# Sorted-block attention before a gated FFN: batch 0 with queries transposed by token halves through an identity selection, keys on split blocks and mixed first, values mixed from strided weight columns

## The chip, the cores and the metric

The kernel runs on one core of a Trainium2 chip. Its metric is the device time of one execution in microseconds (us), lower is better. The core has five engines that run their own instruction streams and wait for one another by semaphores: TensorE (PE, with its weight loads shown apart as PEld), VectorE (DVE), ScalarE (ACT), GpSimd (POOL) and SyncE (SP). Transfers are issued here from POOL's queue (all loads, which also cast from float32 to bf16) and from SP's queue (the outputs and some transposes).

## What is computed

```python
P = sort_net                                   # [4, 8, 8, 8]: batch, head, block i, block j
for _ in range(5):                             # Sinkhorn
    P = exp(P); P = P / P.sum(-1); P = P / P.sum(-2)
k_sorted = einsum('bhij,bhjcd->bhicd', P, k_blocks)    # 8 blocks of 96 tokens, 64 wide
v_sorted = einsum('bhij,bhjcd->bhicd', P, v_blocks)
attn = softmax(q_blocks @ k_sorted.T / 8) @ v_sorted   # inside each block
x = attn with heads side by side                       # [3072, 512]
out = (silu(x @ w_gate) * (x @ w_val)) @ w_out         # 512 -> 1536 -> 512
```

Inputs and output are float32; there are 4 batches, 8 heads, 768 tokens and a head width of 64.

## The kernel before

The work runs batch by batch. A batch gives two token tiles of 384 tokens (half a batch, four blocks), so the FFN has eight tiles, n = 0 to 7. One tile is 12 pairs of `gate` (L351) and `value` (L369), each 4 matmuls of 384 columns into one PSUM bank, and 3 output groups of 12 matmuls (`outp`, L383). The attention of later batches is woven between these by `merge` (L547), which takes a cost for every FFN step and a due time for every side step. That weave is for PE and POOL only; DVE and ACT are ordered there by the framework. Ahead of it, up to L515, the order of PE, POOL, DVE and ACT is written out by hand, and that is the part in question: batch 0 has nothing to hide behind.

For batch 0 the stages are:

- **Loads** (L134 to L152), in POOL's order: the values in two halves, the identity matrix, the queries, the keys in four pieces, then POOL's share of the value copies, then a tiny copy named `landed` (L144) which holds POOL until the last key piece is there, then the FFN weights in steps of 256 columns, batch 1's values, keys and queries, and w_out. Values, keys and queries lie with (head, block j) on 64 partitions each; keys of batch 0 on partitions 0 to 63 and queries on 64 to 127 of one tile.
- **Value transposition** (`copy_v`, L117): POOL and ACT copy the values from "token, width" to "width, token" order into `vch`, so that the 96 tokens of one width column lie next to each other.
- **Sinkhorn** (L183 to L205): five iterations on DVE with an Exp on ACT in each. Between them sit the mask (L187), a copy of the identity into the mixing matrix (L188) and ACT's value copies (L190, L192, L206, L207). PE meanwhile runs matmuls on zeros: `dots(124)` and a few `fill` matmuls of 512 columns per iteration.
- **Mixing matrix**: 16 small matmuls (L432) spread the weights over partitions, and L439 masks them into `rmix`.
- **Mixing** (L449 to L464): `v_chunk` (L238) takes a width column of `vch` as weights and the mixing matrix as the moving operand; `kq_chunk` (L227) takes a token column of the joint key and query tile, so that keys are mixed and queries transposed by the same matmul (the identity part of `rmix`). Each chunk of 8 or 16 columns fills one or two PSUM banks, and DVE ("v") or ACT ("s") drains it to `vt` or `kqt`. PSUM has a two-bank tile "a", a two-bank tile "b", three single banks "gen" and one bank "x".
- **Attention** for units 0 to 3 (L469 to L489): `scores` and `exps` make the exponentials of one head pair and four blocks, `av` multiplies them with the mixed values and DVE divides by the sums (`r_sb` L308, `st` L310), `x_to` transposes the result on PE, and a drain puts it into x of tile 0. One unit gives one of the four 128-row pieces of x for all 384 tokens.
- **First FFN matmuls** (`early`, L492): gate(0), value(0) and gate(1) of tile 0, piece by piece as x arrives.

Thirteen `fill` matmuls (L414) stand between the mixing matrix and the first FFN matmuls. Units 4 to 7 of batch 0 (the tokens of tile 1) are woven into FFN tile 0 (L581), and batch 1 into tile 1.

## Time and profile before

| | |
|---|---|
| median of 3 runs | 250.0 us (249.75 to 250.14) |
| span of the profiled execution | 248.0 us; its own device time is not listed, so 2.0 us to the median stand for what lies around the span |
| PE busy | 240.1 us, 97% of the span, 2636 matmuls |
| DVE, ACT, POOL busy | 157.7, 110.3, 52.5 us |
| chain that ended last, by engine | PE 83%, DVE 7%, ACT 3%, DMA 2% |
| read from HBM | 28.3 MB; the DMA engines are nearly full up to about 85 us |

The span runs from the first to the last instruction, and times inside it are counted from its start. A row of the timeline is: start, length, engine, line, operation, tiles, how many instructions are merged, and in brackets how long the engine had been idle and what ended the wait. A row of the groups gives the busy time and the mean length of one instruction. Matmuls are pipelined, so the length of one says how long it was under way, not how far apart two of them start.

### The profile page before, as it was taken

What the parts mean: (1) busy time and instruction counts of PE and PEld (TensorE: products, weight loads), DVE (VectorE), ACT (ScalarE), POOL (GpSimd) and SP (SyncE); (2) the same over time, 40 slices, a digit from 0 to 9 for tenths busy, and PEclk for the clock granted to TensorE, in tenths of its full rate; (3) what the DMA queues carried; (4) which work ended last, traced back from release to release, by engine and by line L of the source; (5) the groups of instructions that cost most, each with busy time, mean ns of one, the idle gap of its engine ahead of it and who ended that gap; (6) DMA issues with size and microseconds to landing.
All of it is one profiled execution on the core that took longest, in us unless ns stands there. A gap on an engine that the chain in (4) does not pass through costs nothing.

```text
span 248.0 us, 6193 instructions
## 1 busy us (share of the span) xinstructions
PE 240.1 (97%) x2636; PEld 141.3 (57%) x2636; DVE 157.7 (64%) x332; ACT 110.3 (44%) x187; POOL 52.5 (21%) x47
## 2 busy tenths in 40 slices
PE   7899999999999999999999999999999999999994
PEld 6376566666555556655555655565555555555543
DVE  6778689887555775857657646755764585446700
ACT  2977553453544444454642552354244334232311
POOL 7948459960059200000000000000000000000000
PEclk9999999999999999999999999999999999999999
DMA  5959999999999296010122121112111121100122
GB/s 101 211 95 166 215 189 228 194 226 211 221 170 192 53 210 164 3 42 3 45 54 52 57 62 34 44 42 78 32 42 45 39 57 55 42 22 24 42 81 88
DMA packets 39530, 24.38 MB, mean 98 GB/s; under 512 B 27728, under 2 KB 35664, under 8 KB 38992
## 3 DMA queue, kind: packets, MB, share of 16 engines
q0 software_dynamic: 21328, 14.16, 38.9%
q1 hardware_dynamic: 18176, 9.84, 14.1%
q8 instruction: 20, 0.33, 0.5%
q14 instruction: 6, 0.05, 0.1%
HBM read 28.32 MB, written 7.86 MB: 146 GB/s over the span
## 4 chain that ended last, share of the span: by engine, by line
PE 83%; DVE 7%; ACT 3%; issue 3%; DMA 2%; DVEq 0%; ACTq 0%; POOLq 0%
PE v_ps L373 23%; PE o_ps L390 23%; PE g_ps L355 22%; PE tkq L233 4%; PE av_ps L304 3%; PE qk L277 2%; DVE gs_sb L365 2%; DMA v<-in_v_dram 2%; DVE st L310 2%; PE tv L245 2%; PE idle_ps L416 1%; DVE h L378 1%; PE o_ps L406 1%; ACT th_sb L363 1%; PE x_ps L321 1%
## 5 line engine op out<-in xcount | busy, mean ns | idle before, releaser
L365 DVE SCALAR_TENSOR_TENSOR gs_sb<-th_sb,g_ps 128x384 bf16<-128x384 bf16 x96 | 52.8, 550 | 51.8 <-ACT th_sb L363 49.1
L373 PE MATMUL v_ps<-xt,wv_sb 128*128 128x384 bf16 x380 | 77.3, 326 | 0.7 <-DVE gs_sb L365 0.4
L355 PE MATMUL g_ps<-xt,wg_sb 128*128 128x384 bf16 x376 | 76.5, 326 | 0.0
L363 ACT ACTIVATE th_sb<-g_ps 128x384 bf16<-128x384 f32 x96 | 47.1, 490 | 56.0 <-PE g_ps L355 53.5
L390 PE MATMUL o_ps<-wo_sb,h 128*128 128x512 bf16 x276 | 64.0, 379 | 0.0
L378 DVE SCALAR_TENSOR_TENSOR h<-v_ps,gs_sb 128x384 bf16<-128x384 f32 x96 | 53.3, 556 | 6.6
L373 PEld LDWEIGHTS <-wv_sb 128*128 128x128 bf16 x380 | 35.4, 97 | 24.6 <-issue 2.3
L355 PEld LDWEIGHTS <-wg_sb 128*128 128x128 bf16 x376 | 34.6, 97 | 23.2 <-issue 0.3
L390 PEld LDWEIGHTS <-h 128*128 128x128 bf16 x276 | 26.3, 98 | 28.9
L395 ACT COPY o_sb<-o_ps 128x512 f32<-128x512 f32 x23 | 13.5, 585 | 50.8 <-PE o_ps L390 50.8
L124 POOL COPY vch<-v 64x1536 bf16<-64x1536 bf16 (+2 forms) x11 | 28.6, 2639 | 20.7 <-DMA v<-in_v_dram 20.7
L290 ACT ACTIVATE e_all<-qk 96x768 bf16<-96x768 f32 x30 | 22.6, 802 | 8.1 <-PE qk L277 8.1
L310 DVE TENSOR_TENSOR st<-av_ps,r_sb 96x512 bf16<-96x512 f32 x32 | 21.7, 679 | 0.2
L304 PEld LDWEIGHTS <-e_all 96*128 96x128 bf16 x256 | 12.2, 98 | 4.9 <-ACT e_all L290 0.8
L304 PE MATMUL av_ps<-vt,e_all 96*128 96x65 bf16 x256 | 13.5, 194 | 0.0
L211 DVE CAST vt<-tv 96x1024 bf16<-96x1024 f32 (+1 forms) x9 | 9.8, 1100 | 2.7 <-PE tv L255 1.6
L308 DVE RECIPROCAL r_sb<-av_ps 96x8 f32<-96x8 f32 x32 | 6.4, 199 | 7.6 <-PE av_ps L304 7.5
L213 ACT CAST vt<-tv 96x1024 bf16<-96x1024 f32 (+1 forms) x9 | 9.2, 1032 | 3.1 <-PE tv L255 1.8
L211 DVE CAST kqt<-tkq 128x1024 bf16<-128x1024 f32 (+1 forms) x7 | 7.5, 1068 | 2.7 <-PE tkq L233 2.6
L213 ACT CAST kqt<-tkq 128x1024 bf16<-128x1024 f32 (+1 forms) x7 | 6.0, 894 | 6.6 <-PE tkq L233 6.6
L416 PE MATMUL idle_ps<-warm_sb 128*128 128x512 bf16 x28 | 8.7, 409 | 0.0
L233 PE MATMUL tkq<-rmix,kq 128*64 128x64 bf16 x384 | 7.8, 197 | 0.6 <-issue 0.6
(74 smaller groups left out, 126.3 us busy)
## 6 DMA issues: line engine op xcount, KB each, us to landing
out_dram<-o_sb SPq DMA_DIRECT2D x23, 256.0 KB, 2.0
v<-in_v_dram POOLq DMA_DIRECT2D x3, 768.0 KB, 19.9
kq<-in_q_dram POOLq DMA_DIRECT2D x2, 768.0 KB, 13.6
wg_sb<-in_moe_w_gate_dram POOLq DMA_DIRECT2D x6, 256.0 KB, 8.5
wv_sb<-in_moe_w_val_dram POOLq DMA_DIRECT2D x6, 256.0 KB, 9.1
wo_sb<-in_moe_w_out_dram POOLq DMA_DIRECT2D x1, 1536.0 KB, 23.8
kp<-in_k_dram POOLq DMA_DIRECT2D x2, 768.0 KB, 15.1
q_scr<-in_q_dram POOLq DMA_DIRECT2D x2, 768.0 KB, 29.9
```

The lines of the kernel that those rows point to most:

```text
L124: eng.tensor_copy(dst, src.transpose([0, 2, 1]))
L211: nc.vector.tensor_copy(dst, src)
L233: nc.tensor.matmul(tp[two * D:(two + 1) * D, lc, :], lhsT=kq_tiles[b][:, at + lc, :], rhs=rm[:, two], start=True, stop=True)
L290: nc.scalar.activation(e_all[:, n:n + 2, 0:4 * C], wide[0:C, :, 0:4 * C], AF.Exp, scale=scale)
L304: nc.tensor.matmul(o[:, two, i4, :], lhsT=e[:, i4 * C:i4 * C + 128], rhs=vt[:, 2 * g + two, half * 4 + i4, :], start=True, stop=True)
L310: nc.vector.tensor_tensor(st.rearrange("p i two d -> p two i d"), o[0:C, :, :, 0:D], r_sb.to_broadcast([C, 2, 4, D]), op=ALU.mult)
L355: nc.tensor.matmul(g_ps, lhsT=wg_sb[:, kc, ts(m, 128)], rhs=xt[:, kc, :], start=(kc == 0), stop=(kc == NKC - 1))
L363: nc.scalar.activation(th_sb, g_ps, AF.Tanh, scale=0.5)
L365: nc.vector.scalar_tensor_tensor(gs_sb, th_sb, 1.0, g_ps, op0=ALU.add, op1=ALU.mult)
L373: nc.tensor.matmul(v_ps, lhsT=wv_sb[:, kc, ts(m, 128)], rhs=xt[:, kc, :], start=(kc == 0), stop=(kc == NKC - 1))
L378: nc.vector.scalar_tensor_tensor(h_tiles[n][:, m, :], v_ps, 0.5, gs_tiles.pop(m), op0=ALU.mult, op1=ALU.mult)
L390: nc.tensor.matmul(o_ps, lhsT=h_w[:, m, ts(t3, 128)], rhs=wo_sb[:, m, :], start=(m == 0), stop=(m == NFC - 1))
```

## The change

It concerns batch 0 alone, apart from batch 1's value mixing, which now always multiplies all 128 rows, so that the lower half of `vch` is set to zero by POOL.

- **Loads**: first half of the queries (by tokens), the keys in two halves of their 96 tokens on the lower and the upper 64 partitions, the identity, the values as a whole (into a tile with room for 128 tokens, the last 32 set to zero), the second half of the queries, then the FFN weights at once and partly in larger steps. `landed` and all copies of batch 0's values are gone.
- **Queries** (`q0_chunk`): the 384 tokens of one half are 16 runs of 24, so that 8 heads by 16 runs lie on 128 partitions; a matmul on one of the 24 token columns, with identity columns as its moving operand, transposes the heads of one parity. The first half is transposed during Sinkhorn iteration 2 and drained by ACT in iterations 3 and 4; the second half (`q0_rest`) comes inside FFN tile 0.
- **Keys** (`k0_chunk`): 48 token columns with both halves on 128 partitions, mixed by a matrix of twice the width; they come before the values.
- **Values** (`v0_chunk`): the weights are read from the natural tile, 128 tokens with a step of 64 elements.
- **Units 0 to 3** (`blocks`): a unit is now four heads by two blocks, so that units 0 and 1 complete half of the tokens of tile 0 for all heads; the first FFN matmuls run on 192 columns at a time.
- The thirteen `fill` matmuls behind the mixing matrix are gone; the score matmuls of units 0 and 1 stand between value chunks.

The core of the diff (the moved helpers `drain`, `kqt_tile`, `kq_chunk`, `v_chunk` left out):

```diff
-    load_v(0, 0, HC)
-    load_v(0, HC, C)
+    q_runs = q.rearrange("b h (t j c) d -> b t h j (c d)", t=2, c=QC)
+    qk0 = natp.tile([128, C, D], BF16, name="qk0", tag="nat")
+    q0 = [qk0[:, HC + t * QC:HC + (t + 1) * QC, :] for t in range(2)]
+    k0 = qk0[:, 0:HC, :]
+    load_q0(0)
+    for a, rows in enumerate(halves):
+        nc.gpsimd.dma_start(out=k0[rows], in_=k_nat[0, :, a * HC:(a + 1) * HC, :])
     make_identity(nc, ident)
-    load_q(0, 0, C)
-    for lo, hi in ((0, 32), (32, 64), (64, 80), (80, 96)):
-        load_k(0, lo, hi)
-    copy_v(nc.gpsimd, 0, lowr, 0)
-    copy_v(nc.gpsimd, 0, lowr, 3)
-    copy_v(nc.gpsimd, 0, lowr, 5, 8, 40, D)
-    landed = const.tile([R, 1], BF16)
-    nc.gpsimd.tensor_copy(landed, kq_tiles[0][0:R, C - 1, D - 1:D])
-    for m in range(0, 1024, 256):
-        load_gv(m, m + 256)
+    load_v(0, 0, C)
+    nc.gpsimd.memset(v_tiles[0][lowr, C:], 0.0)
+    load_q0(1)
+    load_gv(0, 256)
+    load_gv(256, 512)
+    load_gv(512, 1024)
     load_v(1, 0, C)
-    for m in range(1024, DF, 256):
-        load_gv(m, m + 256)
+    load_gv(1024, DF)
+    nc.gpsimd.memset(vch[lowr, 0:D * C], 0.0)
...
+    def q0_chunk(t, at, n, tag):
+        dst = kqt_tile(0)[:, GI * C:2 * GI * C].rearrange("p (g t r c) -> p t g r c", g=H2, t=2, c=QC)[:, t]
+        sel = ident.rearrange("p (g two r) -> p two g r", g=H2, two=2)
+        tp = chunk_tile("tq0", n // 8, tag).rearrange("p (l g r) -> p l g r", l=n, g=H2)
+        for lc in range(n):
+            for two in range(2):
+                nc.tensor.matmul(tp[two * D:(two + 1) * D, lc], lhsT=q0[t][:, at + lc, :],
+                                 rhs=sel[:, two], start=True, stop=True)
+        return dst[:, :, :, at:at + n], tp.rearrange("p l g r -> p g r l")
+    def k0_chunk(at, n, eng, tag):
...
+                nc.tensor.matmul(tp[two * D:(two + 1) * D, lc].rearrange("p a (g i) -> p a g i", g=H2),
+                                 lhsT=k0[:, at + lc, :], rhs=rm[:, two], start=True, stop=True)
+        drain(eng, dst[:, :, :, at:at + n], tp.rearrange("p l a n -> p a n l"))
+    def v0_chunk(at, n, eng, tag):
...
+            nc.tensor.matmul(tp[:, ld, :], lhsT=v_tiles[0][lowr, :, at + ld], rhs=mix, start=True, stop=True)
+        m = n // len(eng)
+        for k, e in enumerate(eng):
+            part = slice(k * m, (k + 1) * m)
+            drain(e, vts[0][:, 0, :, at + k * m:at + (k + 1) * m], tp[0:C, part].transpose([0, 2, 1]))
...
-        if it == 1:
+        if it == 2:
             with nc.allow_low_precision("0/1 mask"):
-                nc.vector.tensor_reduce(mask, id4, axis=AX.XY, op=ALU.add)
-            nc.vector.tensor_copy(rmix[0][highr, 1].rearrange("p h i -> p (h i)"), ident[highr, highr])
-        if it == 2:
-            copy_v(nc.scalar, 0, lowr, 2, 8)
+                nc.vector.tensor_reduce(mask.rearrange("p a h -> p (a h)"),
+                                        ident.rearrange("p (n j) -> p n j", j=NB), axis=AX.X, op=ALU.add)
         if it == 3:
-            copy_v(nc.scalar, 0, lowr, 3, 8)
+            drain("s", *early_q[0])
+        if it == 4:
+            drain("s", *early_q[1])
...
+        if it == 2:
+            early_q = [q0_chunk(0, 0, 16, "b"), q0_chunk(0, 16, 8, "gen")]
...
-    fill(idle_ps, 1)
-    v_chunk(0, 0, 8, "v", "gen")
...
-    kq_chunk(0, 88, 8, "v", "gen")
...
+    mix_of(1)
+    k0_chunk(0, 8, "v", "gen")
+    k0_chunk(8, 8, "s", "gen")
+    k0_chunk(16, 16, "v", "a")
+    k0_chunk(32, 16, "s", "b")
+    v0_chunk(0, 8, "v", "gen")
+    v0_chunk(8, 16, "v", "a")
+    held = scores(0, 0, "gen")
+    v0_chunk(24, 16, "v", "b")
+    exps(0, 0, *held)
+    v0_chunk(40, 8, "s", "gen")
+    held = scores(0, 1, "gen")
+    v0_chunk(48, 16, "vs", "a")
+    exps(0, 1, *held)
+    mix_of(2)
+    mix_of(3)
+    av(0, 0, "a")
     qk(0, 2, "gen")
...
     av(0, 1, "b")
-    fill(idle_ps, 1)
+    qk(0, 3, "a")
...
+    x_first(0, "s", "x")
+    av(0, 2, "b")
+    x_first(1, "s", "gen")
...
+    early(0, range(NKC), 0)
+    av(0, 3, "a")
+    early(1, range(NKC), 0)
+    x_first(2, "s", "x")
+    early(2, range(NKC), 0)
+    x_first(3, "v", "x")
+    for n in range(3):
+        early(n, range(NKC), 1)
...
-    merge(ffn(0), units(0, range(4, 8), (0.0, 5.6)))
+    def q0_rest():
+        for at, n, eng, tag in ((0, 16, "s", "b"), (16, 8, "v", "a")):
+            drain(eng, *q0_chunk(1, at, n, tag))
+
+    merge(ffn(0), [(0.0, q0_rest)] + units(0, range(4, 8), (1.2, 6.4)))
```

## The prediction

> **What bounds the kernel now.** I read the busy time by stage first (each engine: us busy, instructions in brackets).
>
> ```profile
> core 0: us, PE busy (x) PEld busy (x) DVE busy (x) ACT busy (x) POOL busy (x), PEclk, DMA share, GB/s
> 12.30:20.24 7.94, 7.36 (x263) 5.87 (x263) 6.36 (x8) 5.58 (x9) 4.49 (x8) 1.00 0.74 115
> 20.24:27.24 7.00, 6.91 (x99) 4.17 (x99) 4.43 (x12) 4.85 (x9) 4.60 (x7) 1.00 1.33 174
> 27.24:45.10 17.86, 17.72 (x170) 10.99 (x168) 15.48 (x36) 8.22 (x16) 13.00 (x8) 1.00 1.24 212
> 45.10:246.00 200.90, 198.58 (x1945) 114.64 (x1943) 123.03 (x235) 84.00 (x144) 19.95 (x11) 1.00 0.43 82
> ```
>
> From 27.24 on TensorE (PE) has no gaps worth the name: the stretch of the first token tile is 17.72 busy of 17.86, and all after it 198.58 of 200.90. The change leaves that program alone, so whatever the time before 27.24 gains or loses, plus what is added inside the first tile, arrives at the end undiminished. The two stages before are different: PE looks busy there too, but 13 of its matmuls are fillers (L416). The engines that empty PSUM set the pace, as the timeline shows (start, length, engine, line, count, wait in brackets):
>
> ```profile
> 12.30 1.92 PEld L245 LDWEIGHTS <-vch 64*128 64x128 bf16 x64 [0.23 <-issue]
> 12.30 2.04 PE L245 MATMUL tv<-rmix,vch 64*128 64x64 bf16 x64
> 12.75 2.52 DVE L211 CAST vt<-tv 96x512 bf16<-96x512 f32 x3 [0.59 <-PE tv L245]
> 14.27 2.16 PE L233 MATMUL tkq<-rmix,kq 128*64 128x64 bf16 x112
> 18.18 1.89 DVE L211 CAST kqt<-tkq 128x1024 bf16<-128x1024 f32 x2 [0.99 <-PE tkq L233]
> 19.13 1.01 ACT L213 CAST kqt<-tkq 128x1024 bf16<-128x1024 f32 x1 [1.68 <-PE tkq L233]
> 20.24 0.54 PEld L277 LDWEIGHTS <-kqt 64*128 64x128 bf16 x24 [0.42 <-ACT kqt L213]
> 26.02 0.36 DVE L211 COPY xt<-x_ps 128x384 bf16<-128x384 bf16 x1 [0.47 <-PE x_ps L321]
> ```
>
> Values are mixed from 12.30, keys and queries from 14.27, the last drain ends at 20.14 and scores start at 20.24. The drain of the last piece of x ends at 26.38; I call this moment D. PE still owes 0.86 us of early gate work then, and value(0,1) starts at 27.24 = D+0.86.
>
> Unit prices, from the groups by form of 12 to 27.2 us (behind the bar: us busy, then the mean length in ns):
>
> ```profile
> L310 DVE TENSOR_TENSOR st<-av_ps,r_sb 96x512 bf16<-96x512 f32 x4 | 2.7, 686 | 0.1
> L211 DVE CAST kqt<-tkq 128x1024 bf16<-128x1024 f32 x2 | 2.4, 1224 | 1.1 <-PE tkq L233 1.0
> L213 ACT CAST kqt<-tkq 128x1024 bf16<-128x1024 f32 x2 | 2.0, 1012 | 1.7 <-PE tkq L233 1.7
> L245 PEld LDWEIGHTS <-vch 64*128 64x128 bf16 x64 | 1.9, 95 | 0.2 <-issue 0.2
> L288 ACT ACTIVATE e_all<-qk 96x384 bf16<-96x384 f32 x4 | 1.7, 487 | 0.4 <-PE qk L277 0.4
> L290 ACT ACTIVATE e_all<-qk 96x768 bf16<-96x768 f32 x2 | 1.5, 802 | 0.5 <-PE qk L277 0.5
> L211 DVE CAST kqt<-tkq 128x512 bf16<-128x512 f32 x2 | 1.4, 684 | 0.0
> L213 ACT CAST kqt<-tkq 128x512 bf16<-128x512 f32 x2 | 1.1, 599 | 0.0
> ```
>
> Pace of matmuls: the 64 of L245 take 2.04, less 0.19 for the last one's own length, so 29 ns each; the 112 of L233 17.6 ns. A result is readable 0.2 after its last matmul starts (18.39 + 32 x 0.0176 + 0.2 = 19.15, ACT began at 19.13). Back to back, DVE and ACT instructions overlap by 0.1.
>
> **The change, step by step** (us from the span's start).
>
> *Start of mixing.* The Sinkhorn chain loses a stop: in iteration 1 the mask and the identity copy (0.26 + 0.32 on DVE) held the row sum until 4.61, where the other iterations' spacing gives 4.31. Now the mask sits in iteration 2, between 5.7 and 5.98, when DVE waits for ACT anyway: -0.30. Against it, ACT's drain of the first 16 query columns (1.01) can only start when 32 selection matmuls after the fillers are done, at 8.2, so it ends at 9.22 and the last Exp, due at 9.10, waits 0.1. The mixing matrix now waits for all 16 weight matmuls and is twice as wide: +0.1. The first mixing matmul moves from 12.30 to 12.2.
>
> *Data.* A 768 KB load takes 3.8 on this queue: q landed 9.1 after 2.99, the last key piece 10.8 after 5.1, that is 12.1 and 15.9. In the new order half the queries (384 KB), keys, values, other half, the landings by the same rate are 6.3, 10.1, 14.0 and 15.9; weights follow without the wait on `landed` (L144) and land before FFN(0) wants them. Keys are early by 2. POOL, rid of 6.2 us of copies, has two memsets instead; the first (2048 elements; at POOL's copy price of 2.84 per 1536 at most 3.8) ends before the values land, and batch 1's values land near 30 instead of 34.8, so its second memset hides too.
>
> *Keys.* 96 matmuls, half of one kind of L233: 12.2 to 13.9. Drains 512 and 1024 on DVE (12.7-13.4, 13.5-14.7) and on ACT (12.95-13.55, 14.1-15.1). The order read from the built program says what waits for what from here.
>
> *Values.* If a strided weight column costs what a contiguous one does, v0's first chunk runs at 14.03-14.25. DVE then goes on without rest: 14.65-15.35, 15.45-16.65, 16.55-17.8, and half of the last chunk, 17.7-18.4. The built program makes ACT's half of that chunk wait for DVE's half: 18.4-19.1. Between, scores(0,0) start at 15.25 and ACT does their Exp until 16.5; the Exp of scores(0,1) stand behind the waiting half drain and end at 19.85.
>
> *Attention to D.* av(0,0) 19.1, its st done at 20.5; av(0,1) st 21.35; scores(0,3) wait for tile a until 20.55, Exp to 21.75; av(0,2) st 22.8; the transposes' drains on ACT (0.48 each) end at 22.1 and 22.5. The early gate matmuls, on 192 columns, run in the gaps from 22.2. They delay av(0,3) to 22.7; its st ends at 24.1, the last transpose's drain at 24.9. D moves from 26.38 to 24.9: **-1.5**. The thirteen fillers that go cost nothing where DVE and ACT set the pace. My same rules on the old stretch after 20.24 run up to 0.2 early, so I take **-1.3**.
>
> *What is moved into the first tile.* 48 selection matmuls and two drains now follow value(0,1): 48 x 0.0176 = 0.85 on PE. ACT's drain ends at D+3.25; DVE's drain (0.69) stands behind h(1), starts at D+3.2 and ends at D+3.88. The scores of unit 4 need both, while PE has finished gate(2) at D+3.04: a new stall of 0.9. Together 1.75. But the stretch held slack: from 27.24 to 44.43 PE needs 21 x 0.652 + 2.6 (attention) = 16.3 of 17.19. In the new order DVE catches up during the stall, and following gates and values find their banks free: I get 18.97 from D to the end of value(11) against 18.05, **+0.9**, and 0.15 for the last transpose, now directly ahead of the tile that reads it.
>
> Sum: -1.3 + 0.9 + 0.15 = **-0.25**. The profiled span is 248.0, with 2.0 around it to the median 250.0 (249.75 to 250.14): 247.75 + 2.0 = **249.7**.
>
> *The unknown: strided weight columns.* No row has one. The contiguous ones bound it: L245's loads are 95 ns long but hidden (29 ns pace). Hidden as now, S = 29: nothing. Not hidden at all, S = 95: the last chunk is then ready at 20.7 instead of 17.4 and DVE starts it 3.0 late. Nothing below zero: 29 ns is already the pace of 64-column matmuls. DVE has 0.35 of slack there, so the cost starts near S = 35; at 60 it is 0.9. I take 29 to 35, as every weight load in the trace of 32 to 128 columns is hidden, and keep 95 for the range.
>
> [...]
>
> **Rivals.**
>
> *Strided columns are slow* (the slower side). Place: the 64 loads of v0, 14.0 to 18. Price: -0.25 + 0.9 = +0.65 at S = 60, +2.75 at 95: 250.6 to 252.8. It decides from about S = 55, where the loss passes +0.5. For it: no row with such a load; against it: loads run beside matmuls. Chance 0.20.
>
> *PE's clock falls.* The granted clock reads 1.00 throughout, but fillers tell of two speeds:
>
> ```profile
> 5.23 1.46 PE L416 MATMUL idle_ps<-warm_sb 128*128 128x512 bf16 x3
> 6.90 1.04 PE L416 MATMUL idle_ps<-warm_sb 128*128 128x512 bf16 x4
> ```
>
> Three took 1.46 - 0.2, 0.42 each; later four 1.04 - 0.2, 0.21 each. The change drops 13 fillers, and from 17.2 to 22.2 PE would work only some 1.4 us of 5, with one gap of 1.9. If it fell to the first speed, the FFN would start at half pace; the first rise came about 5 us after PE's first matmul, so 3 to 5 us at half pace lose 1.5 to 2.5: 251.2 to 252.2. Against it: gaps of 0.5 us each iteration did not slow it. Chance 0.15.
>
> [...]
>
> *The first tile takes the moved half for nothing.* If DVE's order leaves no stall and the slack of 0.9 swallows the 48 matmuls, or ACT's half drain does not matter, up to 1.05 comes back: 248.6 to 249.3. For it: slack is there; against: the wait is in the built program. Chance 0.19.
>
> *It does not do what it says:* keys first gains nothing if keys land after 12.2; they have 2 us, so this stands within the forecast.
>
> **How the numbers follow.** Forecast case 0.46, own range 249.1 to 250.3. Bounds: 0.2% is 0.5 us, about what a measurement of this kernel tells from no change: faster is below 249.5, slower above 250.5. The forecast case splits 0.17 / 0.22 / 0.07; the early rival gives faster 0.19; slow columns 0.02 same and 0.18 slower; the clock 0.15 slower. Sums: faster 0.36, same 0.24, slower 0.40. The range takes the low end of the third rival a little further (248.4) and the slow columns up to about S = 85 (252.4); some 0.04 lies below it and 0.12 above.
>
> **What would show it.** Right: first key mixing near 12.2, v0's loads at about 29 ns pace, scores before 16, ACT's half drain starting as DVE's ends near 18.4, the last x drain near 24.9 to 25.1, a PE gap of nearly 1 us ahead of unit 4's scores waiting for DVE's query drain, and everything after 45 unchanged but for a shift. Wrong: v0 matmuls at 60 ns or more; 384-column matmuls at twice 163 ns after 20 us; values landing after 15; a weight matmul in FFN(0) waiting for its load.

## The result, and the profile after

The changed kernel takes **260.43 us** (median of 4 runs, 258.82 to 261.71) against 249.88 us for the kernel before (249.67 to 250.14, 4 runs): a ratio of 1.042, 95% interval 1.037 to 1.047. The forecast was 249.7 us with a range up to 252.4, so it is missed by 10.7 us, and the time lies above its range. The profiled execution took 258.82, the fastest of the four; its span is 257.0 (248.0 before). Below, a run that took over 1.5% longer than the fastest of its kernel (one each of e1_gate and h2_order) is left out.

The same four stages as before, in the changed kernel (each engine: us busy, instructions in brackets, then the granted clock):

```profile
core 0: us, PE busy (x) PEld busy (x) DVE busy (x) ACT busy (x) POOL busy (x), PEclk, DMA share, GB/s
12.30:20.24 7.94, 4.83 (x137) 4.07 (x135) 4.09 (x8) 1.60 (x2) 2.28 (x4) 0.92 1.31 161
20.24:27.24 7.00, 5.52 (x79) 5.26 (x78) 3.90 (x7) 3.00 (x6) 7.00 (x5) 0.50 1.33 204
27.24:45.10 17.86, 16.00 (x215) 11.56 (x214) 12.43 (x27) 9.11 (x17) 11.88 (x5) 0.85 1.11 209
```

The middle stage has a clock of 0.50, the third 0.85, the first 0.92; everywhere in the kernel before it was 1.00. And PE, which was busy 7.36 of 7.94 in the first stage, now works 4.83. Behind 45.10 the clock is 1.00 again, and what follows is only shifted. From PE's first output matmul to the end the span has 189.7 us in both kernels (67.33 to 257.0 after, 58.25 to 248.0 before):

```profile
58.25 1.89 PE L390 MATMUL o_ps<-wo_sb,h 128*128 128x512 bf16 x8
```

```profile
67.33 1.03 PE L444 MATMUL o_ps<-wo_sb,h 128*128 128x512 bf16 x4
```

The last drain of x, the moment D of the prediction, ends at 33.60 instead of 26.38: 7.2 of the 9.0 us. The other 1.9 arise between D and that first output matmul (33.7 against 31.9).

PE in order of time, with its waits in brackets (start, length, engine, line, count):

```profile
9.45 0.95 PE L243 MATMUL tq<-ident,qk 128*64 128x64 bf16 x48 [1.82 <-DMA qk<-in_q_dram]
...
14.00 1.71 PE L253 MATMUL tk<-rmix,qk 128*64 128x64 bf16 x96 [0.38 <-DVE rmix L472]
18.40 2.15 PE L261 MATMUL tv<-rmix,v 64*128 64x64 bf16 x22 [2.69 <-DMA v<-in_v_dram]
...
26.25 0.60 PE L358 MATMUL av_ps<-vt,e_all 96*128 96x65 bf16 x8 [1.48 <-ACT vt L190]
...
38.06 0.52 PE L332 MATMUL qk<-kqt 64*128 64x96 bf16 x16 [1.14 <-DVE kqt L188]
```

Read these against the prediction's times: the early query columns are selected at 9.45, when their load lands; keys are mixed at 14.00 (12.2 was forecast); values start at 18.40, after 2.69 us of waiting for their load (14.03); the first attention waits for ACT's half drain until 26.25 (19.1); the scores of unit 4 wait 1.14 for DVE's query drain. What ACT and DVE did at the places where the chain went through them:

```profile
10.19 1.01 ACT L190 CAST kqt<-tq 128x1024 bf16<-128x1024 f32 x1 [2.58 <-PE tq L243]
11.10 0.20 ACT L281 ACTIVATE p_ps<-p_ps 32x64 f32<-32x64 f32 x1
...
25.53 0.67 ACT L190 CAST vt<-tv 96x512 bf16<-96x512 f32 x1 [1.69 <-DVE vt L188]
```

```profile
24.80 0.69 DVE L188 CAST vt<-tv 96x512 bf16<-96x512 f32 x1 [1.15 <-PE tv L261]
...
33.24 0.36 DVE L188 COPY xt<-x_ps 128x384 bf16<-128x384 bf16 x1 [0.93 <-PE x_ps L375]
...
36.13 0.81 DVE L535 COPY rmix<-ident 64x64 bf16<-64x64 bf16 x1
```

The last Exp of the Sinkhorn loop, due near 9.1, runs at 11.10, behind a drain that could not start before 10.19. ACT's half of the last value chunk (25.53) does wait for DVE's half (24.80 to 25.49), as the built program said. The copy at 36.13 is a 64x64 copy; it comes back below. The weight loads of the values have one line (the mean length behind the comma, ns):

```profile
L261 PEld LDWEIGHTS <-v 64*128 64x128 bf16 x64 | 5.9, 212 | 2.8 <-issue 2.8
```

64 of them take 5.9 us, where 64 contiguous ones took 1.9: this is the strided rival's row. In the timeline 22 start in 2.15 - 0.2, one every 93 ns. The rate of all loads in each of 40 slices of the first 48 us (1.2 us a slice), in the kernel before and then in the changed one:

```profile
GB/s 0 7 97 195 179 265 220 195 181 205 201 200 63 0 20 175 172 114 150 191 198 194 201 195 261 212 256 132 178 195 197 210 283 215 184 256 195 195 161 206
```

```profile
GB/s 0 7 36 102 179 156 201 236 174 241 187 207 136 116 132 186 188 195 198 207 207 208 250 233 199 213 160 202 205 215 286 220 171 236 215 195 167 177 201 212
```

The rate in the steady part is the same, some 200 GB/s. But the start is slower (36 and 102 in the third and fourth slice, where it was 97 and 195), and before, the stream paused from 15 to 17 us, between the last key piece and the first weights; now the weights follow without a pause, while the values are still under way.

### The profile page after: what moved, and what is told of

Read it like the earlier page. It is cut to its first block, busy times and chain, and to the rows that moved or that the text cites. A ratio compares the mean times of both kernels' runs of the same rounds, so it can differ in the third digit from the quotient of the medians.

```text
span 257.0 us, 6177 instructions
## 1 busy us (share of the span) xinstructions
PE 242.2 (94%) x2635; PEld 146.8 (57%) x2635; DVE 158.3 (62%) x330; ACT 105.2 (41%) x183; POOL 49.4 (19%) x39
## 3 DMA queue, kind: packets, MB, share of 16 engines
q1 hardware_dynamic: 18176, 9.84, 13.6%
## 4 chain that ended last, share of the span: by engine, by line
PE 80%; DVE 7%; DMA 6%; issue 3%; ACT 2%; POOL 1%; DVEq 0%; POOLq 0%
PE v_ps L427 22%; PE o_ps L444 22%; PE g_ps L409 21%; DMA v<-in_v_dram 6%; PE av_ps L358 3%; PE qk L332 3%; PE tkq L210 3%; DVE gs_sb L419 2%; PE tv L261 2%; DVE h L432 2%; DVE vt L188 1%; PE o_ps L460 1%; DVE st L364 1%; PE x_ps L375 1%; ACT th_sb L417 1%
## 5 line engine op out<-in xcount | busy, mean ns | idle before, releaser
L444 PEld LDWEIGHTS <-h 128*128 128x128 bf16 x276 | 26.3, 98 | 28.9
L122 POOL COPY vch<-v 64x1536 bf16<-64x1536 bf16 (+1 forms) x8 | 22.4, 2854 | 21.9 <-DMA v<-in_v_dram 21.9
L345 ACT ACTIVATE e_all<-qk 96x768 bf16<-96x768 f32 x29 | 21.9, 802 | 7.8 <-PE qk L332 7.8
L358 PEld LDWEIGHTS <-e_all 96*128 96x128 bf16 x256 | 13.0, 102 | 5.7 <-issue 1.8
L358 PE MATMUL av_ps<-vt,e_all 96*128 96x65 bf16 x256 | 14.2, 200 | 1.6 <-ACT vt L190 1.5
L188 DVE CAST vt<-tv 96x1024 bf16<-96x1024 f32 (+1 forms) x10 | 11.2, 1116 | 7.2 <-PE tv L261 5.2
L190 ACT CAST vt<-tv 96x1024 bf16<-96x1024 f32 (+1 forms) x8 | 8.3, 1034 | 5.4 <-PE tv L232 1.8
L261 PE MATMUL tv<-rmix,v 64*128 64x64 bf16 x64 | 6.1, 268 | 2.7 <-DMA v<-in_v_dram 2.7
L261 PEld LDWEIGHTS <-v 64*128 64x128 bf16 x64 | 5.9, 212 | 2.8 <-issue 2.8
L332 PE MATMUL qk<-kqt 64*128 64x96 bf16 x128 | 5.8, 220 | 1.7 <-DVE kqt L188 1.1
## 6 DMA issues: line engine op xcount, KB each, us to landing
qk<-in_q_dram POOLq DMA_DIRECT2D x2, 384.0 KB, 10.6
```

Source lines behind the costliest of these rows:

```text
L122: eng.tensor_copy(dst, src.transpose([0, 2, 1]))
L188: nc.vector.tensor_copy(dst, src)
L261: nc.tensor.matmul(tp[:, ld, :], lhsT=v_tiles[0][lowr, :, at + ld], rhs=mix, start=True, stop=True)
L345: nc.scalar.activation(e_all[:, n:n + 2, 0:4 * C], wide[0:C, :, 0:4 * C], AF.Exp, scale=scale)
L358: nc.tensor.matmul(o[:, two, n, :], lhsT=e[:, n * C:n * C + 128], rhs=vt[:, 2 * g + two, i, :], start=True, stop=True)
L444: nc.tensor.matmul(o_ps, lhsT=h_w[:, m, ts(t3, 128)], rhs=wo_sb[:, m, :], start=(m == 0), stop=(m == NFC - 1))
```

## Experiments

All times below are medians; the ratio is to seven runs of the kernel before taken beside them, which lie 1.6 to 2.6 us apart. "Values" is the first value mixing on PE, D the end of the last x drain, "half clock" the stretches of the trace's clock records ahead of the last ten us, all in us from the span's start. m1_steps (275.1 us) and m3_loads (78.9) do other work and are read by their rows alone.

| kernel | us | ratio (95%) | values | D | half clock |
|---|---|---|---|---|---|
| before | 249.9 | 1 | 12.30 | 26.38 | none |
| after | 260.4 | 1.042 (1.037-1.047) | 18.40 | 33.60 | 19.0-32.6 |
| e1_gate | 256.3 | 1.025 (1.018-1.032) | 16.02 | 31.26 | 18.6-32.3 |
| e2_drain | 261.1 | 1.041 (1.036-1.047) | 17.63 | 32.99 | 17.4-34.4 |
| e5_gate_drain | 257.9 | 1.031 (1.026-1.035) | 16.36 | 31.66 | 19.6-33.3 |
| e3_contig | 256.8 | 1.023 (1.017-1.029) | 18.62 | 32.78 | 18.5-32.2 |
| b1_strided | 263.2 | 1.051 (1.047-1.055) | 20.49 | 39.06 | 8.1-18.4, 25.2-28.6 |
| b2_strided | 262.1 | 1.049 (1.045-1.053) | 18.60 | 38.30 | 22.6-29.4 |
| b4_strided | 255.4 | 1.020 (1.014-1.025) | 12.07 | 30.81 | 15.6-22.4 |
| e4_fill | 260.5 | 1.041 (1.034-1.048) | 17.49 | 33.27 | 22.1-32.4, 39.2-42.6 |
| b3_nofill | 252.6 | 1.011 (1.008-1.015) | 12.40 | 26.54 | 22.9-26.3 |
| e7_rmix | 258.4 | 1.033 (1.029-1.036) | 17.62 | 33.03 | 17.9-35.0 |
| e6_all | 259.6 | 1.038 (1.031-1.044) | 16.43 | 29.72 | 9.3-12.7, 22.9-29.7, 46.8-50.2 |
| e8_held | 258.6 | 1.033 (1.026-1.040) | 16.27 | 27.07 | 46.8-50.2 |
| e9_later | 260.6 | 1.042 (1.038-1.046) | 16.46 | 27.25 | 54.7-58.1 |
| e10_behind | 259.5 | 1.036 (1.030-1.042) | 16.29 | 28.10 | 18.1-21.5, 59.1-62.5 |
| h1_copied | 260.0 | 1.038 (1.033-1.044) | 19.00 | 34.28 | 10.6-17.4, 24.2-27.6 |
| h2_order | 256.3 | 1.026 (1.021-1.032) | 12.44 | 27.66 | 15.3-18.7 |

**Why the values land late: e1_gate, e2_drain, e5_gate_drain.** In e1_gate POOL reads the end of v0 before it issues the other query half and the weights; e2_drain moves the two early drains; e5_gate_drain has both edits.

```
     nc.gpsimd.memset(v_tiles[0][lowr, C:], 0.0)
+    landed = const.tile([R, 1], BF16)                                    # e1, e5
+    nc.gpsimd.tensor_copy(landed, v_tiles[0][lowr, C - 1, D - 1:D])      # e1, e5
     load_q0(1)
...
-        if it == 3:                                                      # e2, e5
-            drain("s", *early_q[0])
         if it == 4:
+            drain("s", *early_q[0])
             drain("s", *early_q[1])
```

> The changed kernel, with one POOL copy that reads the last element of v0 ahead of the load of the other query half, so that this half and the weights are issued only when v0 has landed. Theory (the loads share the queue, and what is issued behind v0 takes its rate): v0 lands at 13.5 to 14.5 us instead of 18.3, the values are mixed right behind the keys at 15.7, the wait of 2.7 us is gone, PE has no long gap and the clock stays at 1.00: 254 to 256.5 us. Rival (each load has its own slow pace): v0 lands near 18 again, 260 or more.

> The changed kernel, with both early drains of query columns on ACT behind the last Exp of the Sinkhorn loop. The last Exp then runs near 9.1 instead of 11.1 us and the keys can be mixed at 12.2 instead of 14.0. If v0's landing at 18.3 is the later wait, the end doesn't move: 260.0 to 260.9 (the gap on PE only grows to 4.5 us). Rival (the blocked Exp is on the path): 258.4 to 258.9.

> The changed kernel, with the edits of e1_gate and e2_drain together. If both waits are real and stand one behind the other, keys are mixed at 12.2 to 12.6 us and values from 14 to 14.5, and of the 10.5 us that were lost the late start (4.4) and the clock (2 to 3) come back; what is left is the stride: 252.5 to 254. Rival (the drains never cost): the time of e1_gate.

e1_gate is 1.7% nearer to the kernel before, and the values are mixed at 16.02 instead of 18.40:

```profile
16.02 2.11 PE L263 MATMUL tv<-rmix,v 64*128 64x64 bf16 x22 [1.11 <-DMA v<-in_v_dram]
```

So the loads issued behind v0 do take its rate. In these two traces that is worth 2.4 us of landing; over all traces, v0 lands at 17.4 to 18.6 in the five kernels with the loads of the change (after, e2, e3, e4, e7) and at 15.9 to 16.2 in the three with the gate (e1, e5, e6), so the gate is worth 1.1 to 2.7. But without them v0 lands at 16, not at 14 as I expected of e1_gate. The slow start and the end of v0's own transfer are left for the rest; no run separates them. Only e2_drain behaves as expected: the last Exp runs at 9.00, keys are mixed at 12.54, PE then waits 3.38 for v0 instead of 2.69, and the end does not move (the ratio is that of the changed kernel). In its trace D is 0.6 earlier, because v0 landed earlier, and the first tile gives that back (see e7_rmix). e5_gate_drain, too, brings the keys to 12.74 and is no faster than e1_gate. The blocked Exp is a real wait of 2.0 us that costs nothing, because v0 is later still. The clock fell in all three, also where the gap ahead of the values was only 1.1 us (e1_gate). My clock term for these runs was wrong: the long gap alone is not what drops it.

**What a strided load costs: e3_contig, m1_steps, m3_loads.** e3_contig reads 128 contiguous elements instead; m1_steps appends matmuls to the kernel before; m3_loads is a kernel of loads alone.

```
-            nc.tensor.matmul(tp[:, ld, :], lhsT=v_tiles[0][lowr, :, at + ld], rhs=mix, start=True, stop=True)
+            nc.tensor.matmul(tp[:, ld, :], lhsT=v0_flat[:, (at + ld) * C:(at + ld) * C + 128], rhs=mix,
+                             start=True, stop=True)                       # e3
...
+    for step in (1, 2, 4, 8, 16, 32, 64):                                # m1 (96 columns); m3 (128 columns)
+        cols = flat.rearrange("p (n s) -> p n s", s=step)
+        for n in range(32):
+            nc.tensor.matmul(..., lhsT=cols[lowr, 0:96, n % step], rhs=warm_sb[lowr, 0:64], start=True, stop=True)
```

> The changed kernel, with the 64 weight loads of v0's mixing reading 128 contiguous elements each instead of 128 elements that lie 64 apart; the values are then mixed from wrong columns, so the output isn't the reference's; the work and the waits are otherwise the same. Theory (the stride sets a pace of 94 ns): pace 29 to 35 ns at full clock, values done 2.5 to 4 us earlier, 256.5 to 258. Rival (the halved clock or DVE sets the pace there): 260.

> The kernel before, with 224 more matmuls behind its last ones: 32 for each step of 1, 2, 4, 8, 16, 32 and 64 elements between the 96 columns of the weights (64 rows, 64 moving columns), results unused. [...] Rival theory (any step but 1 loses a fast path): 90 ns and more already at step 2. Third (a load of 95 ns is hidden for short steps): 29 ns until step 4.

> None of the computation (the output is zeros): 32 matmuls of 64 moving columns for each step of 1, 2, 4, 8, 16, 32 and 64 elements between 128 weight columns (64 rows), then 128 rows at steps 1 and 64, then 96 columns at steps 1 and 64, with 12 fillers of 512 columns between. [...] Rival (m1_steps was slow for its clock): 96 columns cost 3/4 of 128. Behind that POOL clears 64x6144 twice while DVE does a sum, a 32-bit copy, a 16-bit product and a 16-bit copy of 64x64. Theory (a 16-bit copy from SBUF to SBUF waits for POOL, others don't): only the last takes microseconds. Rival: all wait, or none.

m3_loads gives the price list. Each line is 32 matmuls of 64 columns; the name tells the step in elements, "cols" the loads of 96 columns:

```profile
21.28 1.10 PE L50 MATMUL one<-warm_sb,flat 64*128 64x64 bf16 x32
...
28.75 1.25 PE L50 MATMUL four<-warm_sb,flat 64*128 64x64 bf16 x32
...
32.62 2.11 PE L50 MATMUL eight<-warm_sb,flat 64*128 64x64 bf16 x32
...
42.17 2.19 PE L50 MATMUL thirtytwo<-warm_sb,flat 64*128 64x64 bf16 x32
...
46.99 3.03 PE L50 MATMUL sixtyfour<-warm_sb,flat 64*128 64x64 bf16 x32
...
61.58 1.62 PE L50 MATMUL colsone<-warm_sb,flat 64*96 64x64 bf16 x32
...
65.83 5.43 PE L50 MATMUL colssixtyfour<-warm_sb,flat 64*96 64x64 bf16 x32
```

Take 0.2 off for the last one's own length and divide by 31: 29 ns a load at step 1 (and at 2), 34 at 4, 62 at 8, 64 at 32, **91 at 64**, the step of v0's columns; 128 rows at step 64 take 90. With 96 columns instead of 128 the loads at steps 1 and 64 cost 46 and 164 (the last matmul is 0.34 long there). The 96 columns of m1_steps cost 45 to 47 ns up to step 2, 90 at 4, 176 to 181 at 8 and 16, and 164 at 32 and 64: they rise one step earlier and have no second rise. At steps 4 and 64 the price did not hang on PE's clock: in m1_steps it was halved in the middle of step 4, and the pace stayed at 88 to 91; at 64 it is 164 in both runs, at half clock in m1_steps and mostly at full clock in m3_loads. With 128 columns the price rose from step 4 to 8 (34 to 62) and again from 32 to 64 (64 to 91); what makes these two rises, and the earlier one of 96 columns (47 to 90 from step 2 to 4), nothing here shows.

e3_contig answers for the kernel: a ratio of 1.023 against 1.042 (256.8 us against 260.4). Its profiled run, the slowest of its four, shows less: from the first value mixing to the first attention 6.75 us instead of 7.85, and D 0.8 earlier. It still stands at half clock there, where its contiguous loads go at 53 ns, and PE pauses once for 0.85 for no reason that the profile shows.

**The strided loads alone: b1_strided, b2_strided, b4_strided.** The kernel before with v0 mixed straight from strided columns. Its copies go; three ways of clearing what must hold numbers:

```
+            lhsT=vch[rows, col:col + 128] if b else v_tiles[0][lowr, :, at + ld]       # all three
-    copy_v(nc.gpsimd, 0, lowr, 0)           # and the other two of POOL and four of ACT
+    nc.gpsimd.memset(v_tiles[0][lowr, C:], 0.0)          # b1; on DVE in b2; b4: POOL, once v0's first half has landed
+    nc.gpsimd.memset(vch[lowr, 0:D * C], 0.0)            # b1, b2; b4: v_chunk(1) uses its own 64 rows instead
```

> The kernel before with one part of the change alone: v0 is mixed straight from strided weight columns and its copies on POOL and ACT go (POOL clears the pad of v0 and vch instead). Theory (94 ns a load at 64 elements between the columns): values take 6.0 us on PE instead of 2.0; the drains hide part, so 2.5 to 4 us later from there. If the thin matmuls (27 ns of work in 94) also let the clock fall, half clock somewhere between 15 and 30 us and 2 us more: 252.5 to 254 without, 254 to 257 with the fall. Rival (the stride costs only where PE is already starved): 250 to 250.5.

> The kernel before with the strided weight columns of v0 alone, as b1_strided, but DVE (not POOL) clears the pad of v0, so that DVE's copy of the identity (8.45 us in b1_strided, while POOL cleared) runs before POOL's clearing begins. Theory (94 ns a load): first value mixing near 12.3 as before, 6.0 us of loads instead of 2.0, and the drains hide part: +2.8 to +4.2, or 2 more if the thin stretch lowers the clock: 252.5 to 256. Rival (the copy waits again, for POOL's issuing of loads): near 263.

> The kernel before with the strided weight columns of v0 alone, without the two artefacts of b1_strided and b2_strided: POOL clears the pad of v0 only when v0's first half has landed (6.3 us, where its copies began before), vch isn't cleared at all, and batch 1's values are mixed from their own 64 rows. DVE's copy of the identity should take 0.3 us again. Theory (94 ns a load): value mixing near 12.3, 6.0 us of loads instead of 2.0, scores 2 to 3 us later, and half clock for 3.4 us or more behind the thin stretch: 252.5 to 255. Rival (drains hide it, fillers hold the clock): 250 to 251.

b1_strided took 263.2, slower than the whole change, and not for its loads. DVE's copy of the identity (64x64, 0.32 us before) lasted until POOL had finished clearing (DVE, then POOL, in b1_strided):

```profile
4.16 8.45 DVE L187 COPY rmix<-ident 64x64 bf16<-64x64 bf16 x1
```

```profile
7.27 5.31 POOL L141 MEMSET vch<- 64x6144 bf16 x1
```

7.27 + 5.31 = 12.58 and 4.16 + 8.45 = 12.61. The Sinkhorn chain stood behind it. b2_strided was meant to avoid this and did not (5.70 us, until the clearing of vch ended). Both tell nothing of the stride. b4_strided has the copy at 0.18 and is the clean price:

```profile
12.07 5.89 PE L239 MATMUL tv<-rmix,v 64*128 64x64 bf16 x64
```

64 loads in 5.89 - 0.2, 90 ns each. Scores start at 24.67 instead of 20.24, D is 4.4 later, the kernel takes 2.0% more (1.4 to 2.5%, that is 3.5 to 6.3 us). The clock fell at 15.6, though PE had no gap at all from 12.07 on: the profile counts PE as busy for 4.00 of 4.00 us between 12 and 16, and PEld for 3.94, but 64 matmuls that took 2.04 us in the kernel before were stretched over 5.9, so by these numbers most of that is waiting for weights. m3_loads has the same: its clock fell at 69.11, inside the 5.43 us of 96-column loads at step 64 that started at 65.83.

**The clock: e4_fill, b3_nofill.** Eleven fillers in the wait for v0 of the changed kernel; the 13 fillers of the kernel before taken out.

```
+    idle_ps = bank_tile("idle_ps")                                       # e4
+    fill(idle_ps, 11)
     v0_chunk(0, 8, "v", "gen")
...
-    fill(idle_ps, 4)                        # b3: and the others behind the mixing matrix, 13 in all
     qk(0, 0, "a")
```

> The changed kernel, with eleven 512-column fillers on PE (0.21 us each) in the wait for v0, from 15.7 to 18.05 us. Theory (the empty stretch ahead of v0 is what drops the clock at 18.9): the clock stays at 1.00 and 2 to 3 us come back, 257.4 to 258.4. Rival (the clock falls for the thin work between 20 and 27 us, or from the earlier waits): half clock again within the first 35 us, 260 or more.

> The kernel before without its 13 fillers between the mixing matrix and the first gates; nothing else changes. Theory (the fillers hold the clock): half clock for at least one stretch of 3.4 us between 18 and 32 us, 1.7 us lost for each such stretch in which PE is the bound: 251.5 to 254. Rival (the drains keep PE busy enough): clock 1.00, 249.5 to 250.2.

e4_fill bridged the wait, and the clock held until 22.1 instead of 19.0; then it fell anyway, behind the thin loads, and again at 39.2 behind a wait of 1.94 for DVE. Nothing was gained: the fillers in this one hole did not help; the stretches behind it are thin too (PE is busy for 2.49 of 4.00 us from 24 to 28), and in this trace the first tile lost 2.5 us more than in the changed kernel's (36.2 from D to the first output matmul against 33.7; for the wait see e7_rmix). b3_nofill changes nothing but the fillers. Its scores start at 19.47 instead of 20.24, but from there to D it takes 7.07 us instead of 6.14, so D moved by 0.16 only. The clock fell (the stretch from 24 to 28 us in b3_nofill, with a clock of 0.71 where the kernel before has 1.00; from 20 to 24 it is 0.87):

```profile
24.00:28.00 4.00, 3.95 (x24) 2.23 (x22) 1.71 (x4) 1.66 (x4) 2.17 (x3) 0.71 1.45 194
```

and the time rose by 1.1% (0.8 to 1.5%), 2.1 to 3.6 us. The trace, taken from the fastest run, shows only 0.2 of this up to the first output matmul (58.45); another 1.0 is a later pause of PE that no engine and no load of the profile explains:

```profile
62.22 0.28 PE L233 MATMUL tkq<-rmix,kq 128*64 128x64 bf16 x6 [0.85 <-issue]
```

For the clock as the cause of the rest speaks that the six runs order themselves by their mean clock: 251.3 at 0.991, 252.1 and 252.2 at 0.986, 253.0 at 0.984 and 0.978. The slower ones have no trace, so that the fillers held the clock is shown (1.00 with them, half from 22.9 to 26.3 without), and what the fall costs is in part argued. The half-clock stretches of all traces but those that run into the span's end are 3.41 us long or two to five times that.

**The copy in the first tile: e7_rmix.**

```
+            nc.vector.tensor_copy(rmix[1][lowr, 1].rearrange("p h i -> p (h i)"), ident[lowr, lowr])   # iteration 2
...
     gate_out(0, 1, first[2])
-    nc.vector.tensor_copy(rmix[1][lowr, 1].rearrange("p h i -> p (h i)"), ident[lowr, lowr])
```

> The changed kernel, with DVE's small copy of the identity into batch 1's mixing matrix (64x64) moved from behind the early gates into iteration 2 of the Sinkhorn loop. There it took 0.81 us while POOL's first copy of v1 ran, 0.17 where POOL was idle. Theory (DVE waits for POOL's copy): the wait of unit 4's scores for the query drain shrinks from 1.14 to 0.4 to 0.6, 259.5 to 260. Rival (the stall is the order of DVE's work alone): no change, 260.4.

It took 258.4, faster than the 259.5 to 260 I gave it, but the trace does not put the gain there. Values started 0.8 earlier in that run, which the edit does not cause, and D is 0.6 earlier; from D to the first output matmul it takes 33.8 us, as the changed kernel (33.7). Unit 4's wait fell from 1.14 to 0.27, yet its scores come no sooner behind D (4.52 against 4.46): the clock was halved until 35.0 there, so PE itself was later. With the copy early and the clock at 1.00 (e8, e9, e10, h2) they come at D+4.35 to 4.37, still behind a wait of 1.03 or 1.04; so in the changed kernel's trace the copy costs some 0.1, by an estimate from these. It can cost more. In e2_drain it met POOL's first copy of v1 near its start:

```profile
35.41 11.13 POOL L122 COPY vch<-v 64x1536 bf16<-64x1536 bf16 x4 [6.54 <-DMA v<-in_v_dram]
```

```profile
35.72 2.56 DVE L534 COPY rmix<-ident 64x64 bf16<-64x64 bf16 x1
```

The first of these four POOL copies ends at 38.24, DVE's copy at 38.28, and the scores came at D+6.41. In after, e3 and e4, too, it ends 0.04 behind POOL's copy, after 0.81, 1.25 and 1.61 us; in e1, e5 and e6 POOL was idle, and it took 0.17. That DVE waits for POOL is shown by m3_loads, too, where POOL cleared 64x6144 twice until 11.22 while DVE worked:

```profile
0.74 10.48 POOL L76 MEMSET big<- 64x6144 bf16 x2 [0.29 <-POOLq L100]
```

```profile
6.69 0.62 DVE L78 TENSOR_REDUCE sums<-src 64x1 f32<-64x512 f32 x1
7.23 4.04 DVE L79 COPY copyfull<-src 64x64 f32<-64x64 f32 x1
...
11.95 0.16 DVE L83 COPY copyhalf<-srcb 64x64 bf16<-64x64 bf16 x1
```

The sum (L78) ran in its 0.62; the 32-bit copy behind it (L79) was held until 11.27; a 16-bit copy with POOL idle (L83) took 0.16. So a 32-bit copy was held as well, for 4.04 us, against my expectation; the product and the other copy stood behind the held one, and the run tells nothing of them.

**Do the causes add up: e6_all, e8_held, e9_later, e10_behind.** e6_all joins e1, e2 and e3. e8_held gates on the keys instead, moves the identity copy as e7, and has 15 fillers; e9_later and e10_behind change when batch 1's keys and queries and the output weights are issued.

```
+    nc.gpsimd.tensor_copy(landed, k0[highr, HC - 1, D - 1:D])            # e8, ahead of the weights
+    load_gv(0, 256)
     load_q0(1)
...
+    fill(idle_ps, 4)                        # e8: ahead of v0; 7 ahead of av(0, 0), 2 and 2 behind it
...
+    nc.gpsimd.tensor_copy(landed2, wv_sb[:, NKC - 1, DF - 1:DF])         # e9
     load_k(1, 0, C)                         # e10: these three behind the copies of v1
     load_q(1, 0, C)
     nc.gpsimd.dma_start(out=wo_sb, in_=wo_dram)
```

> The changed kernel, with the edits of e1_gate, e2_drain and e3_contig together (the values come from wrong columns, so the output isn't the reference's). This is the state that the prediction assumed. If late loads, the blocked Exp, the stride and the clock are the whole loss, D is near 25 us and the time 249.2 to 250.8. Rival (something else is lost as well, the moved query half in the first tile above all): 251.5 or more.

> The changed kernel with all that the runs blame taken away at once: weights issued when the keys have landed, the early query drains behind the last Exp, contiguous weight columns for v0 (wrong columns, so the output isn't the reference's), batch 1's identity copy early, and 15 fillers on PE: 4 ahead of v0, 7 ahead of the first attention, 2 and 2 behind it. Theory (these five are the whole loss): clock 1.00 throughout, no wait for a weight in the first tile, 249 to 251. Rival (fillers that push PE don't pay, or something else is lost): 252 or more.

> As e8_held, with batch 1's keys and queries and the output weights issued only when the last weight of the value half has landed (one POOL copy reads it). In e8_held PE waited 1.01 and 3.04 us for weights in the first tile, and the clock was halved for one stretch of 3.4 us behind that. Theory (loads with large packets, issued behind, take the rate of the weights): both waits and the stretch go, 252 to 254. Rival (the queue is simply full): the waits stay, 257 to 260.

> As e8_held (contiguous columns for v0, wrong values), with batch 1's keys and queries and the output weights issued behind POOL's copies of v1 instead of ahead of them, so that neither the weights (e8_held: waits of 1.01 and 3.04 us) nor the copies (e9_later: 4.42) come late. Theory (what the runs found is the whole loss): clock 1.00, no wait over 1.1 us after 30 us, 250.3 to 252. Rival (another wait takes the place): 254 or more.

None reached the forecast, and the theory that the first five causes are the whole loss fell. In e8_held the clock held through the whole attention and D is 27.07, six and a half us better than in the changed kernel. The gain was given back in the first tile:

```profile
41.88 0.82 PE L412 MATMUL g_ps<-xt,wg_sb 128*128 128x384 bf16 x4 [1.01 <-DMA wg_sb<-in_moe_w_gate_dram]
...
45.74 0.82 PE L430 MATMUL v_ps<-xt,wv_sb 128*128 128x384 bf16 x4 [3.04 <-DMA wv_sb<-in_moe_w_val_dram]
```

D + 0.7 against the kernel before, 0.85 for the moved query half, the waits above and one of 1.03 for the moved half's drain, and an estimated 1.7 for 3.41 us at half clock behind the last wait: 8.3, and the span is 8.4 longer. So it adds up, with one cause more: the weights of the first tile came late. e9_later shows why. With the three large loads held back until the last weight had landed, both waits for weights (1.01 and 3.04) were gone: those loads, issued behind the weights, had taken their rate. But holding them held POOL as well, whose copies of v1 stand behind them, and PE waited 4.42 us for vch. e10_behind issued them behind the copies, and PE waited for the queries (2.93) and the output weights (1.89). Each order moved the wait to another load.

**The rest of the change without the stride: h1_copied, h2_order.** v0 is loaded first and copied as before; query halves, split keys and half attention stay.

```
+    load_v(0, 0, HC)
+    load_v(0, HC, C)
     make_identity(nc, ident)
+    load_q0(0)                              # h1; in h2 behind the keys
     for a, rows in enumerate(halves):
         nc.gpsimd.dma_start(out=k0[rows], in_=k_nat[0, :, a * HC:(a + 1) * HC, :])
+    copy_v(nc.gpsimd, 0, lowr, 0)           # and the others of the kernel before; ten fillers
```

> The half of the change that should pay, with the rest as before: queries by halves, split keys and half attention stay; v0 is loaded first and copied to contiguous columns by POOL and ACT as before, values are mixed first, the early query drains follow ACT's copies, weights wait for the keys, the fillers of the kernel before are back, batch 1's identity copy is early. After the start of mixing at 12.2 DVE and ACT empty 9.7 us of drains on two engines instead of 14.6, so scores start near 17.5 instead of 20.24 (-2.7), the moved query half costs 0.9 to 1.2 in the first tile: 248.0 to 249.0. Rival (the attention is held by its own chain or the clock falls): 250 or more.

> As h1_copied, but with the loads in the order v0, keys, query half, and the selection of the queries on PE behind the keys instead of in the Sinkhorn loop, where it held PE until 15.1 us in h1_copied. Theory: values are mixed at 12.2, keys at 14.3, queries when they land near 16; scores near 18.5 instead of 20.24, the moved half costs 1 to 2 us in the first tile: 249 to 250.5. Rival (the thin stretch lowers the clock, or weights come late as in e8_held): 252 or more.

h1_copied shows PE's order as a trap: the selection of the queries stood inside the Sinkhorn loop, its load landed at 13.6, and the mixing matrix behind it on PE came at 18.2. h2_order mends that: scores at 20.54, D 27.66, no better than before at either place, and then waits of 1.03 for the moved half and of 1.65 and 0.42 for weights. It takes 2.6% longer than the kernel before. No version here beats the kernel before.

## Why the prediction was wrong

The prediction's table of D went from 26.38 to 24.9; it became 33.60. Of these 8.7 us, 4.4 are the start of the values (18.40 against 14.03), 2.8 the stretch from there to the first attention (7.85 against 5.1), 1.5 the stretch from there to D (7.35 against 5.8). D and the moved half (0.8 more than forecast) make up the miss of the profiled span, 257.0 against 247.75; the median run is 1.6 us slower than the profiled one and has no trace.

- *Data* (failed, the largest step). "the landings by the same rate are 6.3, 10.1, 14.0 and 15.9"; they were 9.4, 12.5, 18.3 and 19.0. The steady rate was right, the start was slower. What failed is to lay loads one behind the other: they ran side by side, and what was issued behind v0 delayed it (2.4 us by e1_gate, 1.1 to 2.7 over all traces). Half the queries, issued first, landed after 8.1 us. The 2 us by which the keys were to be early became nothing (12.5 against 12.2).
- *Start of mixing* (failed, but off the path). ACT's drain ends at 11.20, not 9.22, because its data was late; the last Exp, "due at 9.10", waited 2.0 instead of 0.1, and the mixing began at 14.0. e2_drain and e5_gate_drain show that this cost nothing while v0 was later. The mask's move did save its 0.3: the second row sum starts at 4.30 (4.61 before), the one behind the mask 0.22 after its Exp, as in the other iterations, and with the drains out of the way the last Exp runs at 9.00 (e2_drain; 9.40 before).
- *The unknown, S* (the value taken failed, the bound was right). I took 29 to 35 ns because "every weight load in the trace of 32 to 128 columns is hidden"; the pace was 93. That contiguous loads hide said nothing of a strided one. The upper bound, 95, came from the length of a hidden load, and fits by chance: a length does not tell a pace, and one strided load is 212 ns long in the profile. Its price at 95, +3.0, is near what e3_contig takes back (1.8% by the ratios, 3.6 us by the medians); in the kernel before, where keys and scores stand behind the values and the clock fell too, the strided loads cost 3.5 to 6.3 us (b4_strided).
- *"The thirteen fillers that go cost nothing"* (failed). They held the clock: without them it fell (half from 22.9 to 26.3 us), and the kernel before took 2.1 to 3.6 us longer (b3_nofill), of which the trace accounts for a part only. In the changed kernel 13.65 us stand at half clock; their price there was not measured by itself. The rival had the right mechanism; its chance of 0.15 was too small, because I looked for one long gap. Here the clock fell without one: in e1_gate with a gap of 1.1 us, in b4_strided with none. I take the prediction's own figure, 1.4 us of work in 5, for the sign; how little work is too little, no run shows.
- *The moved half* (right in kind, too small). From D to the first output matmul 1.9 us instead of 1.05. The stall stands where it was forecast, 1.14 instead of 0.9. In it the identity copy took 0.81 instead of 0.17, because it waited for POOL's copy of v1, which the earlier landing of v1 had moved there; without that the stall is 1.03 (e8_held).
- Right: ACT's half drain waits for DVE's; the thin stretch of PE; nothing changes behind 45 us but for a shift.
- What the forecast left out: the loads fill the queue from 3 to 48 us in both kernels (8.7 MB after, 8.3 before), so an earlier PE needs an order of loads that delays none of them. In e8_held to e10_behind each order tried had one that came late; whether another has none stays open.

## What to carry to other kernels

Lay loads in time by all the bytes that are in flight, not one behind the other, and ask of each load issued earlier which wanted one it slows (here v0 landed at 18.3 us with the other query half and the weights issued behind it, at 15.9 with nothing behind it). That weight loads are hidden in one access pattern (29 ns at step 1) says nothing of another (91 at step 64): price the pattern by itself before data is laid out so that weights are read across it. Fillers on PE held the clock here (1.00 with the 13 of the kernel before, half from 22.9 to 26.3 without them); before some are taken out, look for stretches with little matmul work left, not for long gaps alone (in b4_strided the clock fell with no gap). And before two profiles are compared, look for what differs between them besides the edit: here the landing of v0 (by up to 1.2 us with the same loads) and one small copy (0.17 to 2.56 us).

## What the runs showed of the hardware

- Weight loads of 128 16-bit columns went at 29 ns up to a step of 2 elements, 34 at 4, 62 to 64 from 8 to 32, 91 at 64; with 96 columns 46 at step 1 and 164 at 64 (m3_loads). The halved clock didn't change the pace of 96 columns at steps 4 (88 to 91 on both sides of the fall, m1_steps) and 64 (164 in m1_steps and in m3_loads); 128 contiguous ones went at 53 ns under it (e3_contig).
- The granted clock fell for stretches of 3.41 us or two to five times that (13.65 in the changed kernel). It also fell where PE counts as busy but, by the pace of its matmuls, mostly waits for weights: at 15.6 in b4_strided, inside 5.89 us of loads at 90 ns, and at 69.11 in m3_loads, inside 5.43 us of loads at 164. What makes it fall, these runs don't tell cleanly.
- A 64x64 copy on DVE from SBUF to SBUF was held until POOL's copies or clearings beside it ended: 0.81 us in the changed kernel, 2.56 in e2_drain, 4.04 in m3_loads, 5.70 in b2_strided and 8.45 in b1_strided, instead of 0.16 to 0.32. The 8.45 are longer than either of the two clearings there (1.90 and 5.31). A sum in m3_loads (0.62) and a drain from PSUM in the changed kernel (1.22 beside POOL's clearing of vch) were not.
- Loads on one queue shared the rate while they were in flight: v0 was there at 15.9 with nothing issued behind it (e1_gate) and at 18.3 with the other half and the weights behind it (17.4 in the earliest trace); large loads issued late took the rate of weight loads issued earlier (PE's waits of 1.01 and 3.04 us for weights in e8_held were gone in e9_later, which held those loads back).
